# Low parts of the experts' weights subtracted on VectorE instead of POOL

## The chip, the cores and the metric

The kernel runs on one core of a Trainium2 chip. The metric is the device time of one execution in microseconds. TensorE (PE) multiplies, and its weight loads (PEld) run beside it; VectorE (DVE), ScalarE (ACT) and POOL (GpSimd) work on tiles in SBUF and PSUM; DMA queues move data, those of POOL among them the gathers and scatters by index.

## The reference, cut to what matters

Two parts follow each other: a filter along the sequence by FFT, and a mixture of 8 experts with a greedy, capacity-limited assignment of the 19968 tokens.

```python
X = np.fft.rfft(x, axis=1)                    # x: 8 x 2496 x 256
y = np.fft.irfft(X * (filt_r + 1j * filt_i), n=2496, axis=1)
x = y.reshape(19968, 256)
logits = x @ w_gate                           # 256 x 8
...                                           # greedy: each expert takes 2496 tokens, best logits first
for e in range(8):
    mask = assigned == e
    h = np.maximum(x[mask] @ w1[e], 0.0)      # 256 x 1024
    out[mask] = h @ w2[e]                     # 1024 x 256
```

## The kernel before, in words

The first 530 us are the FFT part. From there on the experts follow each other, some 120 us each, in the order in which the routing settles them. Each expert's 2496 tokens are gathered by index in 20 tiles of 128, transposed on TensorE (`turn`, lines 816 to 832), multiplied by w1 (`first`, line 850, PSUM tiles `pz`), passed through the ReLU, multiplied by w2 (line 899, PSUM tiles `py`) and scattered by index (line 910).

Products are computed with split operands: a tile is rounded to a short format by ScalarE (the high part) and the rounding error (the low part) is computed by a subtraction, so that a product is the sum of high x high, high x low and low x high. This is done for the tokens (`xo` high, `z` low, line 832), for the hidden activations (`hl` holds both, lines 856 to 867) and for the weights (`Ffn.split`). For the weights of one expert, the raw tiles `wr0` and `wr1` (128 x 2048 each, gathered by a DMA of POOL, line 793) give `w0h`, `w0l` (w1) and `w1h`, `w1l` (w2). `split` works on one of eight parts of 128 x 512 each: parts 0 to 3 are w1, whose source is read with a stride of 8 elements, and 4 to 7 are w2. ScalarE casts the high part (line 807), then the low part is subtracted (line 808), with both operands in SBUF.

The weights of expert e+1 are loaded and split while expert e runs. The parts are handed out one by one from the list `split` in `emit`: every `PACE` = 5 yields of TensorE's program one part, and the rest at `flush`. `issue_after(W.lasta)` places a part behind the last ScalarE operation emitted for `hl` or `y`.

The routing of the next experts runs beside it on VectorE, with small matmuls on TensorE and a little ScalarE. `Route.phase` finds thresholds (lines 550 to 610) and prepares the next search (`M`, `tmp`, `ar`, `A`, lines 635 to 645; `asg`, `val`, `r`, `a`, `b`, `dr`, `u`, lines 721 to 734). `Route.places` turns the result into token numbers (`oa`, `OH` at lines 748 and 749, matmuls into `rt` at 755, `loc` at 756, ScalarE's `junka` at 759, `ex` at 760, `js`, `xid`, `t`, `oid` at 763 to 771). PSUM tiles `rt` have 2 buffers, `py` 2, and `pz` and the transposes' `ptr` share 4, so TensorE waits when VectorE or ScalarE has not yet read an older one.

TensorE's order is that of the emission (`manual_schedule`). The order of VectorE, ScalarE and POOL is set by a scheduler when the program is built. Each engine works its queue off in order.

Of the kernel before, what the change touches and what calls it, by code (L numbers as in the profile page):

```python
# [7 lines left out]
F32, F32R = mybir.dt.float32, mybir.dt.float32r  # L8
BF, F16, I32 = mybir.dt.bfloat16, mybir.dt.float16, mybir.dt.int32
AF, OP, AX = mybir.ActivationFunctionType, mybir.AluOpType, mybir.AxisListType  # L10
# [92 lines left out]
class Fft:  # L103
# [150 lines left out]
    def split(s, b, q, v, eng):  # L254
        y = s.yd[b, q] = [s.wp.tile([128, 2, D], F32R, name=n, bufs=3) for n in ("yh", "yl")]
        s.nc.scalar.copy(y[0], v)
        eng.tensor_tensor(y[1], v, y[0].bitcast(F32), op=OP.subtract)
# [517 lines left out]
class Ffn:  # L775
# [19 lines left out]
    def split(s, e, part):  # L795

        nc = s.nc
        raw, hl = s.wt[e]
        k, h = divmod(part, 4)
        src, (hi, lo) = raw[k], hl[k]  # L800
        if k == 0:
            h, j = divmod(h, 2)
            src = src.rearrange("p (j q f) -> p j f q", j=2, f=8)[:, j, 4*h:4*h+4]
            hi, lo = (t.rearrange("p (j f q) -> p j f q", j=2, f=8)[:, j, 4*h:4*h+4] for t in (hi, lo))
        else:
            src, hi, lo = (t[:, 512*h:512*h+512] for t in (src, hi, lo))
        nc.scalar.copy(hi, src)
        (nc.gpsimd if e or part >= 4 else nc.vector).tensor_tensor(lo, src, hi.bitcast(F32), op=OP.subtract)

    def gather(s, e, g, ids):  # L810
        for t in range(4*g, 4*g + 4):
# [109 lines left out]
def emit(tc, i, out):  # L921
    nc = tc.nc
    with ExitStack() as st:
# [82 lines left out]
        while len(split) > 4:  # L1006
            W.split(*split.pop(0))
# [117 lines left out]
```

## Time and profile before

| what | value |
|---|---|
| median of 3 runs | 1605.68 us (1600.03 to 1606.17) |
| the profiled execution | 1590.93 us, its span 1589.2 us |
| busy, share of the span: PE / PEld / DVE / ACT / POOL | 90% / 78% / 63% / 46% / 40% |
| mean granted TensorE clock | 0.955 of full speed |
| line 808 on POOL | 60 subtractions |
| line 808 on DVE | 4 subtractions |

The span runs from the first to the last instruction of the profiled execution, and its time is 1.7 us more. The busy shares are means over the FFT part and the experts; what matters for the change lies where the weights are split, in stretches of about 50 us, one for each expert after the first. These stretches begin at 640, 775, 895, 1015, 1130, 1250 and 1345 us and are called the first to the seventh here.

### The profile page before, as it was taken

To read this page: it belongs to the slowest core of one execution; us is meant where nothing else is said; L and a number is where in the kernel's file an instruction comes from. 1 tells how busy PE (TensorE), PEld (TensorE's weight loads), DVE (VectorE), ACT (ScalarE), POOL (GpSimd) and SP (SyncE) were. 2 spreads that over 40 slices of the span, in tenths; PEclk is the share of its full clock that TensorE was granted. 3 is DMA by queue.
4 is the path that set the end of the run, shared out by engine and by line. 5 is a ranking of instruction groups with operands and counts; after the bars stand their busy time and mean duration, and the time that the engine had idled before them with its cause. 6 is when DMAs were issued, how large, how long until landed. Compare 5 with 4: busy or idle time off the path is not lost.

```text
span 1589.2 us, 27471 instructions
## 1 busy us (share of the span) xinstructions
PE 1422.3 (90%) x10374; PEld 1243.6 (78%) x10374; DVE 997.5 (63%) x2560; ACT 728.1 (46%) x1703; POOL 628.9 (40%) x617
## 2 busy tenths in 40 slices
PE   2688779799888699899999999989989989999998
PEld 2687668689654388788879888879879879899898
DVE  3577556588545866966785787686786772622322
ACT  4465445566444643543542543442543453632322
POOL 0143123335210453464464475453664453633311
PEclk9899889889979799999999999999999999999999
DMA  9878898845778510220221211111211221111100
GB/s 146 146 109 170 188 181 128 172 94 142 192 212 283 179 53 27 80 62 29 84 62 36 70 58 47 74 47 46 86 42 48 85 92 45 45 41 40 51 27 26
DMA packets 121095, 148.74 MB, mean 94 GB/s; under 512 B 70629, under 2 KB 93755, under 8 KB 118659
## 3 DMA queue, kind: packets, MB, share of 16 engines
q1 hardware_dynamic: 97994, 70.63, 22.6%
q0 software_dynamic: 17840, 60.34, 11.8%
q10 hardware_dynamic: 5129, 16.01, 2.9%
q8 instruction: 82, 1.34, 0.4%
q14 instruction: 50, 0.41, 0.1%
HBM read 84.47 MB, written 62.50 MB: 92 GB/s over the span
## 4 chain that ended last, share of the span: by engine, by line
PE 62%; DVE 15%; DMA 8%; issue 6%; ACT 4%; SPq 3%; POOL 1%; POOLq 0%; DVEq 0%; ACTq 0%
PE py L899 20%; PE pz L850 20%; PE pa L271 4%; DMA xt<-x 3%; PE p L222 3%; PE pv L386 3%; PE p L207 3%; PE ptr L828 2%; PE rt L558 2%; PE pa L241 2%; DMA z<-zd 2%; SPq L186 1%; ACT lg L718 1%; PE pv L250 1%; DVE hl L864 1%
## 5 line engine op out<-in xcount | busy, mean ns | idle before, releaser
L899 PE MATMUL py<-w1h,hl 128*128 128x256 f32 x2496 | 488.1, 288 | 8.2 <-DVE hl L867 5.7
L899 PEld LDWEIGHTS py<-w1h,hl 128*128 128x128 f32 x2496 | 405.0, 193 | 12.2 <-DVE hl L867 7.3
L899 PE MATMUL py<-w1l,hl 128*128 128x256 f32 (+1 forms) x1280 | 361.4, 284 | 0.0
L910 POOL DMA_INDIRECT out<-y,oid x160 | 173.8, 1086 | 377.6 <-ACT y L909 335.6
L856 ACT ACTIVATE hl<-pz 128x512 fp32r<-128x512 f32 (+1 forms) x320 | 187.1, 588 | 228.9 <-PE pz L850 207.4
L850 PE MATMUL pz<-xo,w0h 128*128 128x512 f32 (+1 forms) x640 | 266.6, 417 | 14.8 <-DVE hl L864 5.4
L850 PE MATMUL pz<-xo,w0l 128*128 128x512 f32 (+1 forms) x640 | 251.0, 392 | 0.0
L850 PE MATMUL pz<-z,w0h 128*128 128x512 f32 (+1 forms) x640 | 250.2, 391 | 0.3 <-DVE z L832 0.2
L899 PEld LDWEIGHTS py<-w1l,hl 128*128 128x128 f32 (+1 forms) x1280 | 243.4, 190 | 1.9
L864 DVE SCALAR_TENSOR_TENSOR hl<-pz,hl 128x512 fp32r<-128x512 f32 x227 | 155.2, 687 | 129.1 <-ACT hl L856 128.8
L814 POOL DMA_INDIRECT xg<-xs,xid x160 | 168.7, 1055 | 96.7 <-PE ptr L828 33.3
L909 ACT COPY y<-py 128x256 f32<-128x256 f32 x152 | 56.2, 371 | 283.0 <-PE py L899 257.5
L850 PEld LDWEIGHTS pz<-xo,w0h 128*128 128x128 f32 x640 | 123.5, 193 | 35.7 <-DVE hl L864 7.5
L230 POOL TENSOR_TENSOR P<-P 128x256 f32<-128x256 f32 x80 | 59.7, 746 | 210.7 <-DVE P L228 209.6
L207 PE MATMUL p<-cS,xr 117*128 117x120 f32 x688 | 102.5, 295 | 44.2 <-ACT xr L195 30.5
L850 PEld LDWEIGHTS pz<-xo,w0l 128*128 128x128 f32 x640 | 122.1, 191 | 24.2
L215 ACT COPY Y<-p 64x240 f32<-64x240 f32 (+1 forms) x304 | 116.0, 382 | 47.8 <-PE p L207 42.0
L850 PEld LDWEIGHTS pz<-z,w0h 128*128 128x128 f32 x640 | 122.9, 192 | 16.5 <-DVE z L832 1.1
L207 PEld LDWEIGHTS p<-cS,xr 117*128 117x128 f32 x688 | 94.8, 210 | 50.7 <-ACT xr L195 30.5
L550 DVE TENSOR_TENSOR Gm<-M,thr 117x1232 bf16<-117x1232 f32 (+2 forms) x80 | 105.8, 1333 | 0.2
L759 ACT ACTIVATE junka<-rt,loc 128x176 bf16<-128x176 f32 x160 | 65.4, 409 | 69.4 <-DVE loc L756 43.3
L222 PE MATMUL p<-cW,Y 128*128 128x128 f32 x640 | 93.3, 281 | 1.3 <-DVE Q L229 1.3
(235 smaller groups left out, 2371.5 us busy)
## 6 DMA issues: line engine op xcount, KB each, us to landing
xt<-x SPq DMA_DIRECT2D x24, 838.5 KB
zd<-zt SPq DMA_DIRECT2D x140, 128.0 KB
z<-zd SPq DMA_DIRECT2D x26, 600.0 KB
xs<-xo SPq DMA_DIRECT2D x12, 585.0 KB
xs<-xo ACTq DMA_DIRECT2D x11, 585.0 KB
xs<-Y ACTq DMA_DIRECT2D x9, 585.0 KB
zd<-zt ACTq DMA_DIRECT2D x20, 128.0 KB
xg<-xs,xid POOLq DMA_INDIRECT x160, 2.8
```

The lines of the kernel that those rows point to most:

```text
L207: s.lastmm = nc.tensor.matmul(p[:, q-q0, :120], xv[:, q-24*h], s.cS1, start=True, stop=True).ins
L215: (nc.vector.tensor_copy if t in ((5,) if b else (1, 3, 5, 7, 9)) else nc.scalar.copy)(dst, src)
L222: nc.tensor.matmul(p[:, k], s.Y1[b][:, 4*g+k, dh*128:dh*128+128], s.cW[:, 4*g+k], start=True, stop=True)
L271: s.nc.tensor.matmul(p, w, v, start=m == 0, stop=m == 2)
L550: nc.vector.tensor_tensor(Gm[:, s0:s1, :m], s.M[:, s0:s1].unsqueeze(2).to_broadcast([117, s1 - s0, m]), thr[:117].unsqueeze(1).to_broadcas ...
L759: nc.scalar.activation(s.junka, pr[:, h, :S], AF.Sign, bias=loc[:, c:c+1], scale=-1.0, accum_out=js[:, c:c+1])
L814: s.lastg = s.nc.gpsimd.indirect_dma_start(out=xg[:n], out_offset=None, in_=s.xs, in_offset=bass.IndirectOffsetOnAxis(ap=ids[0][:n, t:t+1] ...
L850: nc.tensor.matmul(p[:, :n], w[:, sl], x[:, k, :n], start=m == 0, stop=m == 5)
L856: s.lasta = nc.scalar.activation(h[:, :n], p[:, :n], AF.Relu).ins
L864: nc.vector.scalar_tensor_tensor(l[:, :n], p[:, :n], 0.0, h[:, :n].bitcast(F32), op0=OP.max, op1=OP.subtract)
L899: nc.tensor.matmul(p[:a.stop-a.start], hs[g][f][:, a], b[:, 256*f:256*f+256], start=m == 0, stop=m == 8 * len(terms) - 1, skip_group_check ...
L910: st = nc.gpsimd.indirect_dma_start(out=out_rows, out_offset=bass.IndirectOffsetOnAxis(ap=ids[1][:w, 4*g+t:4*g+t+1], axis=0), in_=y[:w], i ...
```

## The change

The engine of the subtraction at line 808 no longer depends on expert and part: VectorE issues it always. Before, it did so for parts 0 to 3 of the first expert alone. That is 60 of 64 subtractions: 28 of `w0l` and 32 of `w1l`. Places in the emission, tiles and buffers stay.

```diff
         nc.scalar.copy(hi, src)
-        (nc.gpsimd if e or part >= 4 else nc.vector).tensor_tensor(lo, src, hi.bitcast(F32), op=OP.subtract)
+        nc.vector.tensor_tensor(lo, src, hi.bitcast(F32), op=OP.subtract)
```

TensorE's and SyncE's queues stay as they were, word for word. POOL's loses the rows, and the scheduler places them among VectorE's, which moves some of VectorE's and ScalarE's other rows too.

**Order pieces 1.** VectorE's queue in the first stretch, behind `tmp` of line 637, where the last `w0l` of the second expert comes (`wr_6795` is its raw w1, `wr_6796` its raw w2). Before:

```order
L723 SCALAR_TENSOR_TENSOR u_6923<-asg,vc,u 117x176
L550 TENSOR_TENSOR Gm<-M,ic 117x528
L729 TENSOR_TENSOR a_6928<-a_6928,b_6929 128x8
L734 TENSOR_TENSOR r<-r_6664,dr 128x8
L867 SCALAR_TENSOR_TENSOR hl<-pz,hl 128x64
L867 SCALAR_TENSOR_TENSOR hl<-pz,hl 128x384
L756 TENSOR_TENSOR loc<-sidx,rt 128x2
L760 TENSOR_SCALAR ex<-rt 128x4
L749 SCALAR_TENSOR_TENSOR OH<-iota,BC,oa 117x512
L867 SCALAR_TENSOR_TENSOR hl<-pz,hl 128x64
L867 SCALAR_TENSOR_TENSOR hl<-pz,hl 128x384
```

After:

```order
L808 TENSOR_TENSOR w0l<-wr_6795,w0h 128x512
L550 TENSOR_TENSOR Gm<-M,ic 117x528
L723 SCALAR_TENSOR_TENSOR u_6923<-asg,vc,u 117x176
L729 TENSOR_TENSOR a_6928<-a_6928,b_6929 128x8
L734 TENSOR_TENSOR r<-r_6664,dr 128x8
L867 SCALAR_TENSOR_TENSOR hl<-pz,hl 128x64
L867 SCALAR_TENSOR_TENSOR hl<-pz,hl 128x384
L756 TENSOR_TENSOR loc<-sidx,rt 128x2
L749 SCALAR_TENSOR_TENSOR OH<-iota,BC,oa 117x512
L867 SCALAR_TENSOR_TENSOR hl<-pz,hl 128x64
L867 SCALAR_TENSOR_TENSOR hl<-pz,hl 128x384
L808 TENSOR_TENSOR w1l<-wr_6796,w1h 128x512
```

A `w0l` now stands ahead of all of these rows, a `w1l` behind the second pair of line 867, and `ex`, which stood ahead of `OH`, comes behind that.

**Order pieces 2.** VectorE's queue in the fifth stretch, from `tmp` to `ex` (`wr_13164` is the raw w2 of the expert that is split there). Before:

```order
L637 TENSOR_TENSOR tmp<-lg,M 117x1408
L550 TENSOR_TENSOR Gm<-M,ic 117x528
L734 TENSOR_TENSOR r<-r_13031,dr 128x8
L864 SCALAR_TENSOR_TENSOR hl<-pz,hl 128x512
L724 TENSOR_TENSOR asg<-asg,u_13288 117x176
L756 TENSOR_TENSOR loc<-sidx,rt 128x2
L730 TENSOR_TENSOR val<-val,a_13293 128x8
L749 SCALAR_TENSOR_TENSOR OH<-iota,BC,oa 117x512
L760 TENSOR_SCALAR ex<-rt 128x4
```

After:

```order
L637 TENSOR_TENSOR tmp<-lg,M 117x1408
L550 TENSOR_TENSOR Gm<-M,ic 117x528
L864 SCALAR_TENSOR_TENSOR hl<-pz,hl 128x512
L808 TENSOR_TENSOR w1l<-wr_13164,w1h 128x512
L756 TENSOR_TENSOR loc<-sidx,rt 128x2
L771 SCALAR_TENSOR_TENSOR oid<-t1b,t_13184 128x4
L749 SCALAR_TENSOR_TENSOR OH<-iota,BC,oa 117x512
L723 SCALAR_TENSOR_TENSOR u_13288<-asg,vc,u 117x176
L729 TENSOR_TENSOR a_13293<-a_13293,b_13294 128x8
L734 TENSOR_TENSOR r<-r_13031,dr 128x8
L808 TENSOR_TENSOR w1l<-wr_13164,w1h 128x512
L760 TENSOR_SCALAR ex<-rt 128x4
```

Between `tmp` and `ex` two `w1l` have come in; the two rows of lines 724 and 730 moved behind `ex`, and those of 771, 723 and 729 ahead of it.

POOL's queue loses the same rows; its gathers `xg` and scatters `out` follow each other directly where subtractions lay between them.

## Rows read from the trace of the kernel before

**Rows 1.** Split stretches, fourth and sum: busy PE, PEld, DVE, ACT, POOL; granted clock; DMA.
```profile
1015.00:1065.00 50.00, 45.04 (x280) 39.33 (x281) 42.36 (x120) 24.33 (x68) 29.49 (x23) 0.90 0.19 65
...
sum 350.00, PE 317.77 PEld 280.17 DVE 282.29 ACT 198.55 POOL 217.95; mean PE 45.40 PEld 40.02 DVE 40.33 ACT 28.36 POOL 31.14
```

**Rows 2.** TensorE in order of time, with idle time before and its releaser.
```profile
664.65 0.44 PE L850 MATMUL pz<-xo,w0h 128*128 128x448 f32 x1 [1.68 <-DVE ex L760]
...
670.30 0.58 PE L899 MATMUL py<-w1h,hl 128*128 128x256 f32 x2 [2.33 <-DVE hl L867]
...
674.44 0.80 PE L899 MATMUL py<-w1h,hl 128*128 128x256 f32 x2 [1.52 <-DVE hl L867]
...
1043.51 0.79 PE L850 MATMUL pz<-xo,w0h 128*128 128x512 f32 x1 [3.32 <-DVE z L832]
...
1165.03 0.33 PE L755 MATMUL rt<-tab,OH 117*128 117x180 f16 x2 [4.66 <-DVE ex L760]
...
1284.75 1.04 PE L828 MATMUL ptr<-id,xg 128*128 128x128 f32 x4 [4.62 <-DVE hl L864]
...
1368.65 0.38 PE L899 MATMUL py<-w1h,hl 128*128 128x256 f32 x1 [2.34 <-DVE hl L864]
```

**Rows 3.** VectorE in order of time, first stretch, and one row of the seventh.
```profile
649.23 0.75 DVE L749 SCALAR_TENSOR_TENSOR OH<-iota,BC,oa 117x512 f16<-117x512 f16 x1
...
664.57 5.08 DVE L749 SCALAR_TENSOR_TENSOR OH<-iota,BC,oa 117x512 f16<-117x512 f16 x1
...
669.57 0.68 DVE L867 SCALAR_TENSOR_TENSOR hl<-pz,hl 128x64 fp32r<-128x64 f32 x2
...
672.17 1.61 DVE L639 TENSOR_TENSOR tmp<-tmp,val 117x1408 f32<-117x1408 f32 x1
...
673.71 0.67 DVE L867 SCALAR_TENSOR_TENSOR hl<-pz,hl 128x64 fp32r<-128x64 f32 x2
...
1363.28 0.15 DVE L763 TENSOR_SCALAR js<-js 128x4 f32<-128x4 f32 x1
```

**Rows 4.** POOL in order of time, first stretch.
```profile
664.99 1.65 POOL L808 TENSOR_TENSOR w0l<-wr,w0h 128x512 fp32r<-128x512 f32 x1
666.59 2.50 POOL L808 TENSOR_TENSOR w1l<-wr,w1h 128x512 fp32r<-128x512 f32 x2
```

**Rows 5.** The chain of work that ended last, first stretch: start, us, what.
```profile
650.02 1.66 DVE oa L748
...
655.99 1.51 DVE js L763
```

**Rows 6.** Groups by line, all of the kernel: count | busy us, mean ns | idle before.
```profile
L864 DVE SCALAR_TENSOR_TENSOR hl<-pz,hl 128x512 fp32r<-128x512 f32 x227 | 155.2, 687 | 129.1 <-ACT hl L856 128.8
...
L808 POOL TENSOR_TENSOR w0l<-wr,w0h 128x512 fp32r<-128x512 f32 x28 | 49.8, 1777 | 32.3 <-ACT w0h L807 31.9
...
L808 POOL TENSOR_TENSOR w1l<-wr,w1h 128x512 fp32r<-128x512 f32 x32 | 44.1, 1391 | 4.6 <-ACT w1h L807 4.2
...
L808 DVE TENSOR_TENSOR w0l<-wr,w0h 128x512 fp32r<-128x512 f32 x4 | 4.1, 1081 | 2.9 <-ACT w0h L807 2.9
```

**Rows 7.** VectorE in order of time, fourth to seventh stretch.
```profile
1039.17 3.40 DVE L639 TENSOR_TENSOR tmp<-tmp,val 117x1408 f32<-117x1408 f32 x1
...
1156.25 4.78 DVE L637 TENSOR_TENSOR tmp<-lg,M 117x1408 f32<-117x1408 f32 x1
...
1161.58 1.68 DVE L734 TENSOR_TENSOR r<-r,dr 128x8 f32<-128x8 f32 x1
...
1273.84 2.08 DVE L728 TENSOR_SCALAR b<-ev,vc 128x8 f32<-128x8 f32 x1
...
1281.99 1.68 DVE L763 TENSOR_SCALAR js<-js 128x4 f32<-128x4 f32 x1
...
1363.95 1.58 DVE L764 SCALAR_TENSOR_TENSOR xid<-ex,js 128x4 int32<-128x4 f32 x1
...
1366.72 1.27 DVE L770 SCALAR_TENSOR_TENSOR t<-js,ex 128x4 f32<-128x4 f32 x1
```

## The prediction

> **What bounds the kernel now.** I read the page first, then stretches, TensorE's waits, and VectorE and POOL side by side. The matrix engine sets the pace of the second half. The seven stretches of 50 us in which the weights of the experts after the first are split show TensorE busy 317.8 of 350 us, so 32 us of idle time lie exactly there, and VectorE busy 282.3 us, 81% [rows 1]. In the timeline of TensorE its waits of these stretches end on operations of VectorE: `hl` (the low part of the hidden activations), `z` (the low part of the transposed tokens) and `ex` (which frees a PSUM bank of the routing) [rows 2]. TensorE's order is written out by hand, so a late operation of VectorE stops it.
>
> The reader is to see next why VectorE is late. In the first of these stretches an operation `OH` of line 749 takes 0.75 us, and a like one 15 us later 5.08 [rows 3]. POOL works on the low parts at that time: one from 664.99, two more from 666.59 to 669.09 [rows 4]. VectorE's operation ends at 669.65, half a microsecond behind the last of them. The chain of waits runs through such operations: line 748 takes 1.66 us and line 763 takes 1.51 [rows 5], although a line 763 of the same size takes 0.15 elsewhere [rows 3]. In the later stretches the same shows: `tmp` (128x1408 or so) takes 3.40 and 4.78 instead of 1.61, and small ones 1.3 to 2.1 instead of 0.15 [rows 3, 7]. All of these have their operands in SBUF. Line 864, which reads PSUM, keeps 0.69 in the mean of 227 [rows 6]. So I read POOL's subtraction as something that holds VectorE: an operation of VectorE on SBUF that meets one stands until it, and those directly behind it, are over. What the change takes from POOL it gives to an engine which already stands still for a good part of it.
>
> **The change, part by part.** It moves 28 subtractions `w0l` and 32 `w1l` from POOL to VectorE. POOL loses 49.8 + 44.1 = 93.9 us [rows 6]. That by itself is worth nothing: POOL's scatters and gathers wait for others, and no wait in [rows 2] ends on POOL.
>
> *Price on VectorE.* `w0l` stands there already for the first expert: 1.08 us [rows 6], 28 x 1.08 = 30.2 us. `w1l` has the same size and plain rows and isn't shown on VectorE. From above it is bounded by `w0l`, 1.08; from below by the 1408 columns of `tmp` in 1.61 us, so 512 in 0.59 [rows 3]. I take the 0.69 of line 864, which has the same 128x512 [rows 6]: 32 x 0.69 = 22.1 us. In all 52 us, 7.1 for each of the seven stretches. They are not free: VectorE has only 350 - 282 = 68 us of idle time there.
>
> *What is given back* has to be read where TensorE waits, from the new order of VectorE. I take for each such operation the held time ahead of it that goes, and the new L808 rows ahead of it that come.
>
> First stretch, three waits (order pieces 1). The first (1.68 us) is put down to `ex`, but the pair of line 867 just ahead of it reads the PSUM bank that the waiting matmul writes. That pair gets one `w0l` ahead of it and no hold off: +1.1. Ahead of the second (2.33 us), `OH` falls from 5.08 to 0.75: -4.33 + 1.08, 3.2 us earlier, and the wait is gone even though TensorE arrives 1.1 later. The third pair stood behind `tmp` of line 639 (1.61 us) at 673.71 and now stands ahead of it: -4.33 - 1.61 + 1.08 + 0.69, 4.2 earlier; 1.52 us are gone. Sum: +1.1 - 2.33 - 1.52 = -2.7 us.
>
> Fourth stretch (wait of 3.32 us at 1043.51, for `z`): `z` stood behind `tmp` of 3.40 us [rows 7] and stands ahead of it now, behind one `w0l` and one `w1l` more: -3.4 + 1.08 + 0.69 = -1.6; with three tiny operations that it also passes, -2.0.
>
> Fifth (4.66 us at 1165.03, for `ex`, order pieces 2): `tmp` 4.78 to 1.61 and line 734 from 1.68 to 0.15 give -4.7 [rows 7]; one `w0l` and two `w1l` stand ahead, +2.5. Sum -2.2.
>
> Sixth (4.62 us at 1284.75, for `hl`): lines 728 and 763 fall from 2.08 and 1.68 to about 0.2 each [rows 7], -3.4; one `w0l` and one `w1l`, +1.8. Sum -1.6.
>
> Seventh (2.34 us at 1368.65): lines 764, 767 and 770 lie between 1363.95 and 1367.99 [rows 7] where 0.3 would do, -3.7, and no new row ahead of the awaited `hl`: the wait is gone, -2.3. Behind it four `w1l` follow each other, 2.8 us, ahead of the next `hl`; I give 0.8 back. Sum -1.5.
>
> Second and third stretch: operations come earlier and others later in about equal parts; I take 0. The first expert's four `w1l` also go: 2.8 us against holds of the same size; 0.
>
> That is -2.7 - 2.0 - 2.2 - 1.6 - 1.5 = -10.0 us.
>
> *The clock.* The granted clock was 0.90 in the fourth stretch [rows 1], so up to 0.10 x 50 = 5 us are lost in this one, behind a wait of 3.3 us. Between 0 and 10 us could come back, this stretch and as much for the other six together; shorter waits may still bring the lower level. I take -3.
>
> *Waits that the move brings.* VectorE now stands in line for ScalarE's cast of the same part (line 807). POOL stood 31.9 + 4.2 us for it [rows 6]. A wait of VectorE delays all that is queued behind it, `hl`, `z` and `ex` with the rest. In the new order the L808 rows stand later than POOL reached them, and most casts are over by then; I take 0 and keep 36 us as the upper end.
>
> Sum: -10 - 3 = -13 us on a span of 1589.2, in an execution of 1590.9 us. The median of the three runs shown, 1605.7, is 0.9% above it, and the same 13 us are 0.8% of either. **Predicted: 1592 us.**
>
> The Trainium skill has a rule on this, on its page "SBUF — State Buffer", section "Who interferes with whom": a VectorE instruction with two SBUF inputs contends with a GpSimd instruction that reads SBUF, and whoever issued first keeps the shared pair while the other waits for that one instruction. The trace agrees on who is held, but not on the order: `OH` began at 664.57, ahead of POOL's 664.99, and yet was held through three of its operations [rows 3, 4]. By that rule no operation is held for longer than one of POOL's, and the sum is that of the fourth rival.
>
> **The rivals.**
>
> 1. *VectorE waits for the casts* (slower). An L808 row that VectorE reaches before ScalarE has done line 807 stops the routing and `hl` as well. For it speaks that POOL waited 31.9 us for the cast of `w0h`; against it that POOL was idle then and came early. The gain is used up from 13/7 = 1.9 us of such waits for each expert on. All 36 us would give 1605.7 - 13 + 36 = 1629. With two thirds, 1617.
>
> 2. *Nothing changes.* The 52 us of new work take the place of as much held time: the waits stay as long, but end on operations behind an L808 row. For it speaks that the terms above are small differences (4.7 against 2.5). 1600 to 1610.
>
> 3. *The clock comes back too.* If most of the waits go, so do 20 of the 32 us and 8 of the clock: 1605.7 - 28 = 1578.
>
> 4. *Each hold is one operation of POOL*, 1.8 us in the mean of `w0l` [rows 6], and what goes beyond it has another cause and stays. The 5.08 and the 4.78 us then fall by 1.8 only. In the first stretch the third pair comes 4.2 - 2.5 = 1.7 us earlier, which is all that is gained there instead of 2.7; the fifth gains 0.8 instead of 2.2. That is -13 + 1.0 + 1.4 = -10.6 us, 1595. Against it speaks that the 5.08 us end with POOL's third operation and not with its first.
>
> **How the numbers follow.** Less than 0.5% (8 us) can't be told from no change. My forecast (-8 to -20 us) has 0.45, rival 3 has 0.15, rival 4 has 0.08, rival 2 has 0.21, rival 1 has 0.11. Of rival 4 a third, and of the forecast a tenth, falls short of 8 us, which gives faster 0.60, same 0.29, slower 0.11. The range leaves one in ten out at each side: below, most of rival 3, 1575; above, rival 2 with `w1l` at its upper end (five in the sums, 0.4 each: +2 us), 1608.
>
> **What would show it.** In the profile of the changed kernel line 748, 749 and 763 should have means near 0.35, 0.75 and 0.16 us, with no operation of 5 us; `w1l` on VectorE 0.69; the waits at the second and third pair of the first stretch gone, and the first one longer by 1; TensorE idle in the seven stretches some 22 us instead of 32; waits of line 808 for ScalarE on VectorE of a few us in all. I am wrong if the small operations are still held (then POOL's DMA issues hold them), if VectorE waits over 13 us for line 807, or if TensorE's waits keep their sum and end on operations directly behind an L808 row.

## The result, and the profile after

The changed kernel takes 1582.21 us (median of six, 1580.15 to 1591.51), the kernel before beside it 1605.39: a ratio of 0.9865, with a 95% interval of 0.9837 to 0.9894. It is faster, by 1.35% or 21.7 us (17 to 26). The prediction was 1592 us, with a range of 1575 to 1608.

The profiled execution took 1580.15 us, with a span of 1578.4. That of before took 1590.93, less than each of the six timed runs of before (1600 and up). So the two traces differ by 10.8 us only, 3.2 us of which lie ahead of the first matmul of the experts (it starts at 542.5 us before, at 539.3 after), where the change does nothing. Rows of the two can be compared operation by operation; the size of the gain is taken from the timed runs.

One row suggests that the two traces come from chips that differ; on which chip either was taken is not on record. After the change ScalarE stands idle for 9.23 us near 570 us, for an event that the trace calls remote:

```profile
570.82 0.37 ACT L909 COPY y<-py 128x256 f32<-128x256 f32 x1 [9.23 <-remote]
```

Such waits stand in the traces of the sets of runs in which the kernel before takes 1602 to 1606 us, and in none of those in which it takes 1590 to 1592. The trace of before has none and took 1590.93 us; that of after belongs to a set with 1605.39. What ends them is open: in the traces that have them no landing of POOL's DMAs is recorded, so a wait for one would carry this name too.

The stretches first, as in [rows 1] (in each row the busy time of PE, PEld, DVE, ACT and POOL, then the granted clock; the sum is that of all seven):

```profile
1015.00:1065.00 50.00, 44.87 (x304) 39.18 (x303) 41.27 (x132) 28.91 (x77) 18.61 (x16) 0.97 0.23 81
...
sum 350.00, PE 328.51 PEld 291.67 DVE 276.45 ACT 209.75 POOL 142.31; mean PE 46.93 PEld 41.67 DVE 39.49 ACT 29.96 POOL 20.33
```

TensorE's idle time in the seven stretches is 350 - 328.5 = 21.5 us, where it was 32.2. The stretches lie at the same times in both traces while the work in them comes some us earlier after the change, so part of this is a shift: from the experts' first matmul to the last matmul the idle time outside of the stretches rose from 8.2 to 15.2 us. In the fourth the granted clock is 0.97 instead of 0.90. POOL does 75.6 us less there, and VectorE, which took over the work, is busy for 5.8 us less.

The groups by line show why. Before, three small operations that have nothing to do with the change (count, then busy us and mean ns, then idle time ahead):

```profile
L749 DVE SCALAR_TENSOR_TENSOR OH<-iota,BC,oa 117x512 f16<-117x512 f16 x40 | 38.6, 964 | 0.4
...
L748 DVE TENSOR_SCALAR oa<-iota,BC 117x512 f16<-117x512 f16 x40 | 25.4, 636 | 0.5
...
L763 DVE TENSOR_SCALAR js<-js 128x4 f32<-128x4 f32 x40 | 16.4, 411 | 0.0
```

After, the same ones, the moved rows and line 864:

```profile
L864 DVE SCALAR_TENSOR_TENSOR hl<-pz,hl 128x512 fp32r<-128x512 f32 x227 | 155.0, 687 | 121.0 <-ACT hl L856 119.5 <-issue 1.2
...
L808 DVE TENSOR_TENSOR w0l<-wr,w0h 128x512 fp32r<-128x512 f32 x32 | 36.4, 1144 | 10.4 <-ACT w0h L807 7.7 <-issue 2.6
...
L749 DVE SCALAR_TENSOR_TENSOR OH<-iota,BC,oa 117x512 f16<-117x512 f16 x40 | 29.9, 747 | 0.2
...
L808 DVE TENSOR_TENSOR w1l<-wr,w1h 128x512 fp32r<-128x512 f32 x32 | 21.5, 685 | 0.0
...
L748 DVE TENSOR_SCALAR oa<-iota,BC 117x512 f16<-117x512 f16 x40 | 14.1, 353 | 0.3
...
L763 DVE TENSOR_SCALAR js<-js 128x4 f32<-128x4 f32 x40 | 6.7, 169 | 0.0
```

Line 748 falls from 636 to 353 ns, 749 from 964 to 747 and 763 from 411 to 169, and nothing was done to them. Line 864, whose `pz` lies in PSUM, is at 687 ns as in [rows 6]. The moved parts cost 1.144 and 0.685 us each.

VectorE in order of time, in the first stretch, answers to [rows 3]:

```profile
668.49 0.75 DVE L749 SCALAR_TENSOR_TENSOR OH<-iota,BC,oa 117x512 f16<-117x512 f16 x1
...
669.75 0.69 DVE L808 TENSOR_TENSOR w1l<-wr,w1h 128x512 fp32r<-128x512 f32 x1
...
673.69 1.63 DVE L639 TENSOR_TENSOR tmp<-tmp,val 117x1408 f32<-117x1408 f32 x1
```

`OH` of line 749 takes 0.75 us instead of 5.08. TensorE's waits answer to [rows 2]:

```profile
668.67 0.44 PE L850 MATMUL pz<-xo,w0h 128*128 128x448 f32 x1 [2.42 <-DVE loc L756]
...
683.02 0.65 PE L558 MATMUL rt<-A,Gm 117*48 117x96 bf16 x11 [0.51 <-DVE A L645]
...
935.51 0.48 PE L558 MATMUL rt<-A,Gm 117*48 117x64 bf16 x11 [2.90 <-DVE t1b L769]
...
1057.16 0.45 PE L558 MATMUL rt<-A,Gm 117*48 117x48 bf16 x11 [2.02 <-DVE ex L760]
...
1162.76 0.33 PE L755 MATMUL rt<-tab,OH 117*128 117x180 f16 x2 [1.38 <-DVE ex L760]
```

The first wait of the first stretch is 2.42 us instead of 1.68; those of 2.33 and 1.52 us that followed it are gone, as are those of the sixth and seventh stretch (4.62 and 2.34), and near 1043 0.50 us are left of 3.32. In the fifth 4.66 us became 1.38. In the third stretch a new one of 2.90 us stands, for the routing's `t1b`, where one of 2.12 us for `ex` went (924.72 us before); the 2.02 us in the fourth stood there before as 1.54 (1058.49).

### The profile page after: what moved, and what is told of

It is laid out like the page before. It is cut to its first block, busy times and chain, and to the rows that moved or that the text cites. A ratio compares the mean times of both kernels' runs of the same rounds, so it can differ in the third digit from the quotient of the medians.

```text
span 1578.4 us, 27475 instructions
## 1 busy us (share of the span) xinstructions
PE 1419.3 (90%) x10374; PEld 1240.7 (79%) x10374; DVE 979.5 (62%) x2620; ACT 727.5 (46%) x1703; POOL 537.5 (34%) x557
## 4 chain that ended last, share of the span: by engine, by line
PE 43%; DVE 10%; issue 7%; ACT 2%; POOL 1%; DMA 1%; another core or an unknown queue 0%; POOLq 0%; DVEq 0%; ACTq 0%
PE py L899 20%; PE pz L850 19%; PE rt L558 2%; PE ptr L828 2%; DVE hl L864 1%; POOL out L910 1%; ACT lg L718 1%; DVE hl L867 1%; DVE w0l L808 1%; DVE w1l L808 1%; DMA wr<-moe_w,widx 1%; DVE Gm L550 1%; DVE OH L749 1%; PE rt L755 1%; DVE tmp L639 0%
## 5 line engine op out<-in xcount | busy, mean ns | idle before, releaser
L222 PEld LDWEIGHTS p<-cW,Y 128*128 128x128 f32 x640 | 82.9, 194 | 7.8 <-issue 3.7
```

The costliest lines, as they stand in the source:

```text
L222: nc.tensor.matmul(p[:, k], s.Y1[b][:, 4*g+k, dh*128:dh*128+128], s.cW[:, 4*g+k], start=True, stop=True)
```

## The experiments

Each kernel was timed beside the kernel before on the same chip, and only the ratio is compared across sets, since the kernel before itself had medians between 1590 and 1606 us in these sets. "Held" below is the sum, over VectorE's operations from 540 us on that ran while a POOL operation of the named line did, of the time by which each was longer than the quick quarter of its own form (0.15 us or more). Rows in which the timeline merges several operations are left out; with each operation taken by itself the sums 59.4, 63.8 and 27.5 are 59.8, 71.2 and 33.7. The busy times are those of the first part of each page. Where an edit inserts lines behind line 808, later lines have higher numbers in that kernel's rows.

| kernel | us | ratio to before, interval | VectorE busy, us | TensorE busy, us | held by the part in question, us |
|---|---|---|---|---|---|
| before | 1605.39 | 1 | 997.5 | 1422.3 | 59.4 (line 808 on POOL) |
| the change | 1582.21 | 0.9865, 0.9837 to 0.9894 | 979.5 | 1419.3 | 0 |
| POOL subtracts too | 1628.53 | 1.0254, 1.0228 to 1.0280 | 1050.7 | 1433.9 | 63.8 |
| POOL writes numbers | 1562.58 | 0.9823, 0.9787 to 0.9860 | 982.5 | 1418.8 | 2.1 to 4.9 |
| w0l alone moved | 1581.18 | 0.9940, 0.9923 to 0.9957 | 999.4 | 1420.8 | 32.9 (w1l) |
| w1l alone moved | 1571.87 | 0.9898, 0.9867 to 0.9929 | 985.7 | 1420.7 | 32.6 (w0l) |
| the change again | 1584.60 | 0.9873, 0.9843 to 0.9903 | 980.6 | 1420.6 | - |
| neither subtracts | 1563.54 | 0.9737, 0.9717 to 0.9757 | 938.7 | 1415.9 | 2.8 |
| VectorE subtracts twice | 1615.43 | 1.0072, 1.0046 to 1.0098 | 1027.6 | 1428.1 | 0 |
| line 860 on VectorE too | 1583.08 | 0.9851, 0.9831 to 0.9870 | 987.8 | 1417.6 | 0 |
| POOL copies | 1592.50 | 1.0001, 0.9981 to 1.0022 | 1016.0 | 1423.6 | 27.5 |
| w0 in plain order | 1601.81 | 1.0068, 1.0045 to 1.0090 | 969.4 | 1467.4 | - |
| w2 gathered by rows | 1624.29 | 1.0145, 1.0118 to 1.0172 | 969.6 | 1438.4 | - |
| the same, 8 buffers for y | 1557.08 | 0.9798, 0.9772 to 0.9824 | 968.5 | 1413.8 | - |

**POOL subtracts too.** The theory is that of the prediction: while POOL subtracts, VectorE's operations on SBUF stand still. The rival is that the gain came from POOL's queue or from earlier low parts.

```diff
         nc.vector.tensor_tensor(lo, src, hi.bitcast(F32), op=OP.subtract)
+        if e or part >= 4:
+            d = s.ww.tile([128, 512], F32, name="wd", bufs=1)
+            d = d.rearrange("p (f q) -> p f q", q=4) if k == 0 else d
+            nc.gpsimd.tensor_tensor(d, src, hi.bitcast(F32), op=OP.subtract)
```

> After the change, with the 60 subtractions also done a second time by POOL into a scratch tile that nobody reads. Theory (VectorE's operations on SBUF wait while POOL subtracts): VectorE's busy time goes up from 979.5 by about the 59 us of held time that the trace of before showed, to 1030 to 1060, single operations of 4 to 5 us stand beside POOL's line again, TensorE idles over 30 us in the seven stretches, and since VectorE also keeps its own 52 us of subtractions the time is 1605 to 1630. Rival (the gain came from freeing POOL's queue, or from low parts that are ready earlier): VectorE stays at 980, its operations keep their lengths, and the time is within 0.5% of 1582.

VectorE has the same operations in the same order as after the change, and its busy time went from 979.5 to 1050.7. VectorE and POOL in order of time, in the first stretch:

```profile
672.55 2.54 DVE L749 SCALAR_TENSOR_TENSOR OH<-iota,BC,oa 117x512 f16<-117x512 f16 x1
...
673.00 1.54 POOL L812 TENSOR_TENSOR wd<-wr,w0h 128x512 f32<-128x512 f32 x1
674.62 1.62 POOL L812 TENSOR_TENSOR wd<-wr,w1h 128x512 f32<-128x512 f32 x1
```

`OH` takes 2.54 us again. It began ahead of POOL's operation, and it ends 0.5 us behind the end of the first one, inside the second. Besides the routing the moved subtractions were held themselves (15.3 of the 63.8 us). The rival's numbers did not come, and VectorE's busy time lies in the theory's range. Two other numbers of the theory missed: no operation is held for more than 2.3 us where 4 to 5 were expected, and the ratio of 1.0254 is above its range (1630 on 1605 is 1.015). POOL's queue holds its subtractions again here, but of TensorE's waits from 540 us on all but 1.2 us (for ScalarE's `y`) end on VectorE: the operations of POOL, and not its queue, bring back the long rows. That none is as long as 5 us fits the rows: before, POOL's subtractions followed each other without a gap [rows 4] and `OH` ended behind the third; here 0.08 us lie between them (674.54 to 674.62), and `OH` gets in there.

**POOL writes numbers.**

```diff
+        if e or part >= 4:
+            d = s.ww.tile([128, 512], F32, name="wd", bufs=1)
+            for _ in range(3 if k == 0 else 2):
+                nc.gpsimd.iota(d, [[1, 512]], base=0, channel_multiplier=0, allow_small_or_imprecise_dtypes=True)
```

> After the change, with POOL writing 3 (parts of w0) or 2 (parts of w1) index patterns of 128x512 into a scratch tile at each of the 60 places: POOL is busy for 1.1 to 1.7 us there as before, but it reads no SBUF. Theory in its narrow form (only an operation of POOL that reads tensors from SBUF holds VectorE): busy time of VectorE 980, time 1580 to 1590. Wider form (any POOL operation on SBUF holds it): VectorE at 1030 or more, time 1600 to 1630 as in the run with both subtractions. Rival (POOL's queue alone mattered): the time rises to 1590 or more with VectorE at 980.

VectorE's busy time stayed at 982.5. One of these pairs in the first stretch, with VectorE's operation beside it:

```profile
647.58 1.30 POOL L812 IOTA wd<- 128x512 f32 x2
...
647.83 0.75 DVE L749 SCALAR_TENSOR_TENSOR OH<-iota,BC,oa 117x512 f16<-117x512 f16 x1
```

`OH` keeps its 0.75 us. The narrow form of the theory holds, with a reserve: nothing makes the index numbers wait for the weights, so POOL ran all of them between 459 and 769 us and not at the 60 places; what they would do in the later stretches was not seen. Of the 4.9 us in the table 2.8 belong to operations that ran beside POOL's subtraction of line 860 as well. The Trainium skill says of this, on its page "SBUF — State Buffer", section "Who interferes with whom", that a VectorE instruction with two inputs in SBUF contends with a GpSimd instruction that reads SBUF, and not with one that only writes; the row of 0.75 us agrees.

**POOL copies.** One tensor read instead of two, into the same scratch tile.

```diff
+            nc.gpsimd.tensor_copy(d, src)
```

> After the change, with POOL copying the same part of the weights (one tensor read from SBUF, one written) into a scratch tile at the 60 places. The run with two operands read brought VectorE's busy time from 980 to 1051 us and the ratio to before to 1.025; the run with POOL only writing left it at 982 and at 0.982. If any read of SBUF by POOL holds VectorE, VectorE's busy time is 1030 or more, the lines 748, 749 and 763 have means of 0.55, 1.0 and 0.34 us again, and the ratio is 1.01 or more. If it takes two operands, VectorE stays near 982 and the ratio near 0.985. In between (1000 to 1020), the held time goes with the time that POOL spends on it.

It came out in between, with 27.5 us held in 37 operations by 61.2 us of copies, where 96.7 us of subtractions held 63.8 in 49. VectorE and POOL in the first stretch:

```profile
648.22 1.45 DVE L748 TENSOR_SCALAR oa<-iota,BC 117x512 f16<-117x512 f16 x1
...
648.35 1.15 POOL L812 COPY wd<-wr 128x512 f32<-128x512 f32 x1
```

Line 748, which has one tensor as input, takes 1.45 us instead of 0.35, and begins ahead of the copy. So POOL needs no second operand for the effect, and the outcome is not cleanly one of the three forms of the copy's expectation. VectorE's 1016 us lie in the third; of the long means of the first one is back (line 748 with 0.571 us) and two are not (lines 749 and 763 with 0.795 and 0.179). A us of copying held VectorE for 0.45 us, a us of subtracting for 0.66.

**One kind alone.** The condition picks the engine by part.

```diff
-        nc.vector.tensor_tensor(lo, src, hi.bitcast(F32), op=OP.subtract)
+        (nc.gpsimd if part >= 4 else nc.vector).tensor_tensor(lo, src, hi.bitcast(F32), op=OP.subtract)
```

leaves `w1l` on POOL (`w0l` alone is moved), and

```diff
-        nc.vector.tensor_tensor(lo, src, hi.bitcast(F32), op=OP.subtract)
+        (nc.gpsimd if e and part < 4 else nc.vector).tensor_tensor(lo, src, hi.bitcast(F32), op=OP.subtract)
```

leaves the 28 of `w0l` there (`w1l` alone is moved).

> Only the 28 strided parts of the first weights (w0l) go to VectorE; the 32 parts of w1l stay on POOL. Theory: the held time comes back for the w1l part alone. By busy time on POOL of before that is 44.1 of 93.9 us, so about half of the gain is left: 1592 to 1597, and in the first stretch, where the waits stood beside w1l parts (664 to 669 us), TensorE's waits of 1.5 to 2.3 us behind L867 are back. Rival (only one of the two kinds mattered, the strided one): 1582.

> Only the 32 parts of w1l go to VectorE; the 28 strided parts of w0l from the second expert on stay on POOL. Theory: about half of the gain, 1590 to 1595, and the long operations of VectorE stand only beside w0l parts. Since a w0l part costs VectorE 1.14 us and held it for at most POOL's 1.78, while a w1l part costs it 0.69 against 1.39, the parts of w1l are the better half to move: this run should be no slower than the one with w0l alone. Rival (the w0l parts are the whole gain): 1605.

Each kind is worth something alone, 0.6% and 1.0%, and the held time that is left lies beside the other kind only. The groups by line, of the first kernel:

```profile
L749 DVE SCALAR_TENSOR_TENSOR OH<-iota,BC,oa 117x512 f16<-117x512 f16 x40 | 35.3, 883 | 0.2
...
L748 DVE TENSOR_SCALAR oa<-iota,BC 117x512 f16<-117x512 f16 x40 | 14.9, 373 | 0.3
```

and of the second:

```profile
L749 DVE SCALAR_TENSOR_TENSOR OH<-iota,BC,oa 117x512 f16<-117x512 f16 x40 | 34.3, 857 | 0.4
...
L748 DVE TENSOR_SCALAR oa<-iota,BC 117x512 f16<-117x512 f16 x40 | 26.8, 670 | 0.5
```

With `w1l` on POOL line 749 stays long and 748 is short; with `w0l` on POOL both are long. Moving `w1l` gives more for less: 32 x 0.685 = 21.9 us of work remove 59.4 - 32.6 = 26.8 us of held time, while 28 x 1.144 = 32.0 us for `w0l` remove 59.4 - 32.9 = 26.5. The waits behind line 867 that were expected back in the first stretch with `w1l` on POOL were not: one of 0.38 us stands there, and one of 2.46 for `loc`.

**The price of both sides.** The changed kernel once more, one in which neither engine subtracts, and one in which VectorE does it twice.

Neither subtracts (the work is left out, and POOL writes index numbers into the low parts):

```diff
-        nc.vector.tensor_tensor(lo, src, hi.bitcast(F32), op=OP.subtract)
+        if e or part >= 4:
+            nc.gpsimd.iota(lo, [[1, 4], [4, 128]] if k == 0 else [[1, 512]], base=0, channel_multiplier=0, allow_small_or_imprecise_dtypes=True)
+        else:
+            nc.vector.tensor_tensor(lo, src, hi.bitcast(F32), op=OP.subtract)
```

VectorE subtracts twice:

```diff
         nc.vector.tensor_tensor(lo, src, hi.bitcast(F32), op=OP.subtract)
+        if e or part >= 4:
+            nc.vector.tensor_tensor(lo, src, hi.bitcast(F32), op=OP.subtract)
```

> The changed kernel itself once more, beside the kernel before and beside the other runs. The ratio to before is 0.9865 again within its interval (0.984 to 0.989). With before at 1590, as it was on this chip in the last runs, that is 1568. TensorE's idle time in the seven stretches should be 20 to 23 us again. If the ratio comes out nearer to 0.992 (13 us), the forecast sum was right and the first measurement large by chance.

> The subtraction is left out: at the 60 places POOL writes index numbers into the low parts (about 0.57 us each), so that neither POOL reads there nor VectorE does the work. This gives the bottom for the whole change. Theory: 52 us less work on VectorE than after the change, VectorE's busy time near 925, and as the new work costs TensorE something, the time is 5 to 20 us below the changed kernel. If it is within 3 us of it, VectorE's new work is wholly hidden and the gain of the change is all that the held time ever cost.

> VectorE does each of the 60 subtractions twice, POOL none. This prices VectorE's work at these places without any held operation: 28 of 1.14 and 32 of 0.69 us, 54 us in all. If work on VectorE cost as much as held time, the kernel would lose at least what the change gained, 1590 to 1605. Theory: it costs less for each us than the held time did, since it stands at places at which the emission has room, and the time is 1575 to 1590 where the changed kernel has 1568. Rival (it is hidden): under 1573.

These four stand in one set, with before at 1606.21. Held time alone: 1606.2 - 1563.5 = 42.7 us for 59.4 us held, 0.72 us each. Work alone: 1584.6 - 1563.5 = 21.1 us for 28 x 1.144 + 32 x 0.685 = 53.9 us, 0.39 each. The same work once more: 1615.4 - 1584.6 = 30.8 us, 0.57 each. The gain of the change is the difference of two large terms, 42.7 and 21.1. They also fit the run in which POOL copies: 53.9 x 0.39 + 27.5 x 0.72 = 41 us over the kernel in which neither subtracts, 2.6%, and the ratios differ by 1.0001 - 0.9737 = 2.6%. They do not fit the one in which POOL subtracts too: 53.9 x 0.39 + 63.8 x 0.72 = 67 us, 4.2%, for 5.2% measured; why it is more there stays open. By VectorE's busy time, in which neighbouring operations overlap, it is nearer to one price: 42.7 us for 997.5 - 938.7 = 58.8 (0.73), 21.1 for 980.6 - 938.7 = 41.9 (0.50), 30.8 for 47.0 (0.66). VectorE's work is not hidden here. The expectation for the doubled work missed: it had 7 to 22 us for it, and the 30.8 lie in what it had set for work that costs as much as held time. The 21.1 us are just above the 5 to 20 that had been expected, and they hold more than VectorE's work, since index numbers wait for no cast of ScalarE's.

Held time has a second price, with VectorE's order kept, from the two runs in which POOL works on top of the change: (1.0254 - 0.9869) x 1606 = 62 us for 63.8 held, and (1.0001 - 0.9869) x 1606 = 21 us for 27.5, 0.97 and 0.77 each, on other chips than the change was timed on. So held time comes out at 0.7 to 1.0 and work at 0.4 to 0.6; by busy time the two nearly meet, and that a held us costs more than a worked one is likely, but not shown. A reason for it (held time comes in lumps of some us, which a buffer of two cannot cover) is an argument only.

In the kernel in which neither subtracts one operation speaks against the narrow form of the theory:

```profile
799.17 2.01 DVE L763 TENSOR_SCALAR js<-js 128x4 f32<-128x4 f32 x1
...
799.55 2.13 POOL L809 IOTA w0l<- 128x512 fp32r x4
```

This `js` took 2.01 us instead of 0.16 beside index patterns, which read no tensor. It is most of the 2.8 us held in that kernel.

**Line 860.** POOL's other subtraction, of 29 low parts of the hidden activations, goes to VectorE and PSUM as well.

```diff
-            if f % 2 == 1 and f < 7 and 0 < g < 4 and s.busy():
+            if False:
```

> After the change, with the other subtraction of POOL gone too: the 29 low parts of the hidden activations that line 860 did on POOL are done by VectorE from PSUM, as the other 227 are. POOL's 45 us and ScalarE's 29 additional operations of 0.59 us go, VectorE gets 29 of 0.69, 20 us, and loses the 9.6 us by which its operations were still longer beside line 860. Theory: a low part from PSUM on VectorE is not held itself, so the sum is near nothing: within 0.5% of the changed kernel, VectorE's busy time 990. Rival (the work on VectorE is what is short now): 5 to 10 us slower than the changed kernel.

0.9851 beside 0.9873 in the same set: no difference that can be told. The held time beside line 860 is 9.6 us after the change and gone here, and 29 x 0.69 = 20 us of work came for it. The prices of 0.72 and 0.39 say the same: 9.6 x 0.72 = 6.9 us of held time against 20 x 0.39 = 7.8 us of work.

**Cheaper parts.** `w0l` costs 1.144 us where `w1l`, of the same size, costs 0.685, since its source is read in steps of 8 elements; ScalarE's cast of it costs 1.194 against 0.621. First, the columns were left in the order in which they come:

```diff
-            src = src.rearrange("p (j q f) -> p j f q", j=2, f=8)[:, j, 4*h:4*h+4]
-            hi, lo = (t.rearrange("p (j f q) -> p j f q", j=2, f=8)[:, j, 4*h:4*h+4] for t in (hi, lo))
+            src, hi, lo = (t[:, 1024*j+512*h:1024*j+512*h+512] for t in (src, hi, lo))
...
-                sl = slice(1024*k+128*f, 1024*k+128*f+128)
+                sl = slice(1024*k+f, 1024*k+1024, 8)
```

> After the change, with the first weights left in the order of columns in which they come: the cast and the subtraction read and write 512 neighbouring columns, and the weight loads of line 850 take every eighth column instead. From the rows of w1, VectorE's w0l falls from 1.14 to 0.69 us (32 of them, 15 us less) and ScalarE's w0h from 1.19 to 0.62. By the price of VectorE's work that the runs with none and with twice the work gave (0.4 to 0.6 us for each us) the kernel gains 5 to 9 us over the change, a ratio to before of 0.981 to 0.984. Rival: weight loads over every eighth column are slower than the 188 ns of before; there are 1920 of them, so 100 ns more each are up to 190 us, and the kernel is far slower. A second rival: the first matmul of an expert now needs all four parts of its low weights instead of two, and waits of some us at the start of an expert use the gain up.

The groups by line, after the change:

```profile
L850 PEld LDWEIGHTS pz<-xo,w0l 128*128 128x128 f32 x640 | 121.4, 190 | 24.1
```

and with the plain order:

```profile
L849 PEld LDWEIGHTS pz<-xo,w0l 128*128 128x128 f32 x640 | 213.0, 333 | 0.4
...
L849 PE MATMUL pz<-xo,w0l 128*128 128x512 f32 x512 | 209.3, 409 | 0.0
...
L807 DVE TENSOR_TENSOR w0l<-wr,w0h 128x512 fp32r<-128x512 f32 x32 | 21.7, 687 | 7.0 <-ACT w0h L806 7.0
```

The first rival had it: a weight load over every eighth column takes 333 instead of 190 ns. The 1920 loads of line 850, in three groups of 640, take 636 us instead of 366, 270 us more. Most of that lies beside the matmul before, but not all: matmuls of 397 ns in the mean take 409, and TensorE's busy time rose by 1467.4 - 1419.3 = 48.1 us. VectorE's part did fall to 0.687.

Second, the order was settled by the gather of w2, by rows, which leaves both sides plain (the lines of `split` change as in the first edit, and a second column of `widx` holds the rows' index):

```diff
-        s.w2 = i['moe_w2'].rearrange("e (q f) d -> (e q) (f d)", f=8)
+        s.w2 = i['moe_w2'].rearrange("e f d -> (e f) d")
...
+            for f in range(8):
+                r = nc.gpsimd.indirect_dma_start(out=raw[1][:, 256*f:256*f+256], out_offset=None,
+                    in_=s.w2, in_offset=off[1], element_offset=128*256*f).ins
```

> After the change, with the order of the hidden columns settled by the gather of the second weights instead of by the split of the first: partition q takes the rows q, 128+q, 256+q and so on of w2, in 8 gathers of 128 KB for each expert where there was one, and one VectorE operation more for each expert makes their index. Then both the split of w0 and the weight loads of line 850 run over neighbouring columns. VectorE's w0l falls from 1.14 to 0.69 (15 us in all), ScalarE's w0h from 1.19 to 0.62 (18 us), TensorE's weight loads stay at 190 ns and its busy time at 1419 instead of 1467. By the price of VectorE's work (0.4 to 0.6 us for each us) it gains 6 to 9 us over the change: a ratio to before of 0.981 to 0.983. POOL issues 56 gathers more at about 1.0 us. Rival: POOL, which gathers the tokens and scatters the outputs, is late by these, or weights of 1 KB a row arrive late, and the ratio is 0.987 or more.

It was slower by 1.45%. POOL, ScalarE, VectorE and TensorE in order of time, in the third stretch, the idle time ahead in brackets:

```profile
911.33 0.99 POOL L796 DMA_INDIRECT wr<-moe_w,widx  x1 [0.30 <-issue]
...
921.39 0.95 POOL L798 DMA_INDIRECT wr<-moe_w,widx  x1 [0.30 <-issue]
922.64 1.00 POOL L916 DMA_INDIRECT out<-y,oid  x1 [0.30 <-issue]
...
925.67 0.37 ACT L915 COPY y<-py 128x256 f32<-128x256 f32 x1 [8.10 <-remote]
...
926.58 0.69 DVE L870 SCALAR_TENSOR_TENSOR hl<-pz,hl 128x512 fp32r<-128x512 f32 x1 [7.17 <-ACT hl L862]
...
927.32 1.01 PE L834 MATMUL ptr<-id,xg 128*128 128x128 f32 x3 [6.07 <-DVE hl L870]
```

Nine gathers follow each other from 911.33 to 922.34 us. The scatter behind them starts at 922.64, ScalarE waits 8.10 us to write `y` (its buffers are read by scatters), `hl` stands behind that for 7.17 and TensorE for 6.07. The rival's place was right: POOL's queue. One number mends it:

```diff
-                y = s.wp.tile([128, D], F32, name="y", bufs=4)
+                y = s.wp.tile([128, D], F32, name="y", bufs=8)
```

> The run with the gather by rows once more, with 8 buffers instead of 4 for the output tile y. In that run POOL issued the 8 gathers of w2 one behind the other from 911.33 to 922.34 us, the scatter of an output stood behind them, ScalarE waited 8.10 us for a free y, and line 870 and TensorE behind it, 6.07 us. Theory (the 8 gathers block the scatters, and these the four y): with 8 buffers ScalarE goes on, its waits for y go, and the ratio to before falls from 1.0145 to 0.981 to 0.990. Rival (the tokens' gathers, which stand in the same queue, are late too, or weights in rows of 1 KB come late): TensorE's waits for xg and for the cast of w1 stay, and the ratio stays above 1.0.

0.9798: this version is 2.0% faster than the kernel before, a little more than expected. It was not timed beside the change, whose ratios of 0.9865 and 0.9873 come from other chips; by these it would be about 0.7% ahead of that. Its groups by line:

```profile
L915 ACT COPY y<-py 128x256 f32<-128x256 f32 x152 | 56.5, 372 | 294.4 <-PE py L905 272.4 <-PE rt L571 18.9 <-DMA out<-y,oid 2.6
...
L814 DVE TENSOR_TENSOR w0l<-wr,w0h 128x512 fp32r<-128x512 f32 x32 | 21.7, 685 | 6.2 <-ACT w0h L813 6.2
```

In the run with 4 buffers ScalarE stood 30.1 us ahead of `y` for an event that the trace calls remote, 9.2 us of the kind after the change; here 2.6 us for the scatters' transfers are left. Part of that may be the chip: this set has the kernel before at 1591 us, and in such sets the kernels with 4 buffers show no remote wait either. `w0l` costs 0.685. What 8 buffers would give without the other gather was not tried, so what lies between this version and the change is not split between the two.

## Why the prediction was right, point by point

*The mechanism* was right. All means that were named came in: 353, 747 and 169 ns for lines 748, 749 and 763 (0.35, 0.75 and 0.16 us forecast), no operation of 5 us, and the runs with POOL subtracting or copying bring long rows back, with VectorE's order the same as after the change. That POOL's DMA issues hold these operations is excluded: they all stayed.

*The price on VectorE*: 28 x 1.144 + 32 x 0.685 = 53.9 us for a forecast of 52. The source of `w0l` for the first expert (1.08) was 6% low, the guess for `w1l` from line 864 right within 1%.

*The waits.* The second and third wait of the first stretch went and the first grew, by 0.74 us for +1.1. In the fourth the wait for `z` went. In the fifth 3.3 us went where 2.2 were forecast, in the sixth all 4.6 where 1.6 were, in the seventh 2.3 where 1.5 were. In the second and third, forecast at 0, TensorE's busy time fell by 0.9 and 0.6 us; the 2.90 us for `t1b` are part of that. In the seven stretches TensorE's idle time fell by 10.7 us for a forecast of 10.0, but this agreement is in good part luck. The same kernel, profiled again, had 350 - 323.4 = 26.6 us of it, where 20 to 23 had been expected, and idle time outside of the stretches rose by 7.0 us. From the experts' first matmul to the last matmul the kernel before, the change, and the run in which POOL writes numbers have these sums:

```profile
542.50:1584.20 1041.70, 1001.30 (x6971) 893.16 (x6971) 660.92 (x1885) 438.52 (x1018) 487.82 (x417) 0.98 0.17 54
...
539.30:1573.40 1034.10, 997.43 (x6971) 890.20 (x6971) 644.91 (x1945) 438.03 (x1018) 396.95 (x357) 0.99 0.17 55
...
542.70:1555.30 1012.60, 989.11 (x6971) 885.17 (x6971) 645.62 (x1945) 438.79 (x1018) 471.86 (x481) 1.00 0.17 56
```

Idle time is 40.4 us before, 36.7 after (39.5 in the second profile) and 23.5 where POOL writes numbers. Only the last trace is of a set like that of the trace of before, with nearly the work of the change on VectorE; there 16.9 us of idle time went. So each wait is read rightly for the most part, and the sum of -10 is not shown.

*The clock.* -3 us were taken; TensorE's busy time, which holds what the clock costs, fell by 1422.3 - 1419.3 = 3.0 us, by 1.7 in the second profile. In the part of the experts alone it fell by 3.9 us after the change, rose by 1.4 in the second profile, and fell by 12.2 where POOL writes numbers (granted clock 1.00 instead of 0.98). What the clock gave stays open.

*ScalarE's casts.* VectorE stood 7.7 us in all for line 807, where 0 was taken with 36 as the upper end. That lies under the 13 us from which rival 1 would have decided.

*The sum was too small*: -13 us, while the timed runs give -21.7 and, the second time, -21.6 (1606.2 - 1584.6), outside of the likeliest case's -8 to -20. The step that mis-sized it is the one that gave back only what TensorE waited for in seven windows of 50 us, with 0 for two of them. The runs put it in two larger terms: all held time cost 42.7 us and the work that replaced it 21.1. The forecast compared the two row by row and met their difference only where a wait was seen. The bare sum over VectorE, 59.4 us held against 52 of work, would have given 7 us and no more; what was missing is a price for each of the two, for which the trace of before has no row. The result lies in the range because the rivals had made it wide; at its lower end the text counts most of rival 3 as below 1575, while its own sum puts that at 1578.

*Rival 2* fell, since the time changed by far more than its interval; but it was right that the work is not free. *Rival 3* is nearest in time (1578). Whether for its reason is open: the changed kernel's own traces show no 8 us from the clock, and the run in which POOL writes numbers has 16.9 and 12.2 us for its 20 and 8. *Rival 4* fell with [rows 3, 4]: of 44 held operations of the kernel before 32 met one of POOL's subtractions, but 12 met two or three, and `OH` was held through three. The run in which POOL subtracts too has no operation held through three of POOL's, but one through its first into the second. *Rival 1* fell.

## What to carry to other kernels

When VectorE is short and POOL computes on SBUF beside it, add up how much longer VectorE's operations are than the quick ones of their own form; that time is paid by VectorE, and the move pays when it is more than the moved work costs there. Work of POOL that reads no tensor held VectorE next to nothing here (one operation of 2.01 us), and line 864, which reads PSUM, was not held at all (687 ns before and after). Look at the source's steps before moving anything, and when a queue gets more DMA issues, count the buffers that its later entries set free.

## What was not expected

- A step of 8 elements (32 bytes) in the source makes an operation 1.7 to 1.9 times as long on three engines: VectorE 1.144 against 0.685 us, ScalarE 1.194 against 0.621, TensorE's weight load 333 against 190 ns.
- An operation whose record begins ahead of POOL's is held nevertheless: 0.45 us ahead in the run in which POOL subtracts too (672.55 and 673.00), 0.13 us ahead beside a copy (648.22 and 648.35).
- The kernel before had medians from 1590.0 to 1606.2 us on different chips, 1%, almost as much as the change is worth.
